# Reordering the head of an attention and MLP block: norms ahead of weight scaling, first keys on ScalarE, a shared bank for later keys, gate products as single steps

## The chip, the cores and the metric

The kernel runs on one core of one Trainium2 chip. The metric is device time in microseconds (us), the median of several executions. Before the change it was 1155.14 us (three runs, 1154.14 to 1156.71). The profiled span is about 2 us shorter than the device time of the same run (1153.5 us against 1155.31 for the kernel before).

## The reference, cut to what matters

One transformer block over 2048 tokens of 1024 channels, with adaptive layer norms, multi-query attention (32 query heads, one key and value head of 32 channels) and a gated MLP of width 3584.

```python
mod = (silu(c) @ w_mod).reshape(...)             # sa, ca, ga, sb, cb, gb: six rows of 1024
h = layernorm(x) * (1 + ca) + sa
q, k, v = h @ wq, h @ wk, h @ wv                  # k and v: one head for all 32 query heads
x = x + ga * (softmax(q k^T / sqrt(32)) v @ wo)
h = layernorm(x) * (1 + cb) + sb
x = x + gb * ((silu(h @ w1) * (h @ w3)) @ w2)
```

## The kernel before

The kernel builds a graph of instructions, each with a priority and a stated duration. A list scheduler in the program then fixes one static order for each engine, and picks a bank of PSUM (where the kernel's matmuls put their results) for each group. Copying a result out of PSUM is called evacuating it; a tile is 128 tokens. A lower priority number goes first, and `bp` below is subtracted from it.

The parts that the change and the argument touch:

```python
# eight PSUM banks: PB[0], PB[1], and six that the scores use (PB[2..7] = SP[0..5])
def kproj(t0, n, allow=None):                     # keys of n tokens, replicated on four row groups
    ...
    g = mm_group(NC, kmm, lambda c: [("WKS", 0)] + hk(c, t0, n), n_cols=n, allow=allow, mode="V", prio=KP)
    G.add("dve", lambda e, g=g: e.tensor_scalar(KT[:, sl], PB[g.bank][:, 0:n], BIA[:, 0:1], None, ALU.add), ...)

EV = (("act",), ("act",), ("dve",), ("dve",))     # who evacuates the transposes of tiles 0-3, 4-7, ...
def ln(t):
    bp = -3 if t >= 8 else 0                      # priority of a tile's statistics and norm
...
kproj(0, 256, (2, 3, 4, 5))
qproj(0, 256, 0, (2, 3, 4, 5), prio=1)
kproj(256, 256, (6, 7))
kproj(512, 512, (6, 7))                           # keys of tiles 4 to 7: in a bank of the scores
...
def gate(m, scale):                               # rows ga and gb, for all tokens: wide products
    ...
            def mm(e, kb=kb, sl=sl, g=g):
                for k in range(4):
                    i = e.matmul(PB[g.bank], SCB[kb * 4 + k], WMS[:, sl, k, :], ...)   # 128x512
            G.add("pe", mm, ..., dur=4 * MM, ...)
...                                               # columns sb and cb: 16 small products in one step
            def mm(e, kb=kb, h=h, sl=sl, g=g):
                for k in range(4):
                    for j in range(4):
                        i = e.matmul(PB[g.bank][:, h * 4 + j:h * 4 + j + 1], WMS[:, sl, k, j * P:(j + 1) * P], ...)
            G.add("pe", mm, ..., dur=16 * 0.06, ...)
...
def step(f, s):                                   # one score step: 4 heads x 256 keys x 256 queries
    parts = [(0, 2, 2 * ((2 * i) % 3), 2), (2, 2, 2 * ((2 * i + 1) % 3), 2)]   # its 4 score banks
    G.add("pe", smm, ...)                         # 8 matmuls, then two exponentials of 128x1024 on ScalarE
    G.add("act", ... e.activation(U[...], SP[:, b0:b0 + nb, 0:W], ACT.Exp, scale=SCALE), ...)
...
G.warm = (WARM, MM, warm, ident, 26.0)            # until WARM = 250 us: spare TensorE time is filled
```

The last line is about warm-up matmuls: where the scheduler sees TensorE idle, it inserts products with the identity matrix, whose results nobody reads; they are meant to keep TensorE's clock up.

The softmax here doesn't subtract the row's maximum and nothing guards it: scores larger than these inputs give would overflow.

## Time and profile before

| stretch | what bounds it |
|---|---|
| 0 to 34 us | loads (DMA share 1.09 from 14 to 24 us) and the chain to the first scores; ScalarE waits for keys |
| 34 to 1040 us | ScalarE's 1024 exponentials, TensorE about equally busy |
| 1036 to 1153 us | TensorE alone: the rest of one MLP, one output projection and one whole MLP |

There are 512 score steps, each followed by two exponentials. Below, "exponential n" is the n-th in time, and the "tail" runs from the start of the last score step to the end of the span.

Time by stretches, before. After the stretch and its length come each engine's busy time with its instruction count (PE is TensorE, PEld its weight loads, DVE VectorE, ACT ScalarE), then the granted TensorE clock, the DMA engines' share and GB/s.

```profile
150.00:200.00 50.00, 46.45 (x562) 19.78 (x560) 46.98 (x74) 47.09 (x51) 3.30 (x4) 0.97 0.06 18
300.00:350.00 50.00, 46.52 (x691) 28.38 (x683) 41.52 (x60) 48.69 (x54) 3.40 (x4) 0.97 0.70 176
350.00:1000.00 650.00, 644.81 (x9269) 444.40 (x9269) 607.99 (x879) 646.70 (x735) 12.20 (x20) 1.00 0.68 189
```

From 350 to 1000 us TensorE and ScalarE are both 99% busy. TensorE is less busy from 188 to 192 us (2.14 of 4) and from 330 to 335 us (1.67 of 5), and the mean clock of the two stretches of 50 us around these places drops to 0.97.

ScalarE's timeline in the head, before, with the start, the length, the instruction, and in brackets the idle time ahead of it and what ended it (L930 is line 930 of the kernel's source):

```profile
25.75 2.13 ACT L745 ACTIVATE WREG<-WO,MODC 128x384 bf16<-128x384 bf16 x4
27.79 1.91 ACT L930 ACTIVATE UREG<-SP 128x1024 bf16<-128x1024 f32 x2
33.66 12.09 ACT L930 ACTIVATE UREG<-SP 128x1024 bf16<-128x1024 f32 x13 [3.96 <-PE SP L920]
```

The first two exponentials run, then ScalarE waits 3.96 us for the second score step. TensorE's timeline in the same stretch:

```profile
27.03 0.40 PE L920 MATMUL SP<-QT,KT 32*128 32x256 bf16 x8
27.36 0.39 PE L637 MATMUL SP<-HREG,WKS 128*32 128x512 bf16 x1
28.99 0.40 PE L637 MATMUL SP<-HREG,WKS 128*32 128x512 bf16 x3 [1.24 <-issue]
29.32 0.75 PE L762 MATMUL PB<-SAB,WO 128*128 128x1 bf16 x24
29.93 0.35 PE L768 MATMUL PB<-QT,SAB 128*128 128x32 bf16 x8
30.21 1.69 PE L637 MATMUL SP<-HREG,WKS 128*32 128x512 bf16 x28
31.84 1.05 PE L658 MATMUL PB<-HREG,WREG 128*128 128x256 bf16 x8
...
33.21 0.40 PE L920 MATMUL SP<-QT,KT 32*128 32x256 bf16 x8
```

L920 is a score step, L637 keys, L762 and L768 bias products, L658 queries. Between the two score steps stand the keys of tiles 4 to 7 (L637, 512 columns), which occupy a score bank, and a gap of 1.24 us that no wait in the profile explains ("issue").

The place near 330 us, TensorE's timeline and two stretches, before:

```profile
330.48 0.40 PE L920 MATMUL SP<-QT,KT 32*128 32x256 bf16 x8
332.31 0.40 PE L920 MATMUL SP<-QT,KT 32*128 32x256 bf16 x8 [1.43 <-ACT UREG L930]
334.14 0.40 PE L920 MATMUL SP<-QT,KT 32*128 32x256 bf16 x8 [1.44 <-ACT UREG L930]
335.01 1.53 PE L1146 MATMUL PB<-QT,HREG 128*128 128x256 bf16 x9 [0.47 <-DVE QT L1129]
```

```profile
330.00:335.00 5.00, 1.67 (x46) 0.64 (x37) 5.00 (x14) 5.00 (x7) 0.00 (x0) 1.00 0.83 226
335.00:340.00 5.00, 4.99 (x40) 2.99 (x41) 3.50 (x4) 4.32 (x7) 0.00 (x0) 0.66 0.68 216
```

Two score steps have nothing else between them. TensorE is busy 1.67 of 5 us, and in the next 5 us the granted clock is 0.66. The trace's clock record has it at one half for exactly 3.413 us, from 335.6 to 339.0, also from 192.3 to 195.7, and again from 1151.4 to the end of the span.

### The profile page before, as it was taken

Reading aid. Unit: us, or ns where it says so; the run is one execution under the profiler, and the core shown is the slowest. Engines: PE = TensorE matmul, PEld = TensorE weight load, DVE = VectorE, ACT = ScalarE, POOL = GpSimd, SP = SyncE. Lnnn points to the kernel's source line nnn. Section 1 sums busy time; section 2 is a strip of 40 time slices with the busy share of each in tenths; the row PEclk is TensorE's granted clock in tenths of the full one; section 3 lists DMA queues with packets and bytes.
Section 4 is the critical chain, followed back from the end, with each engine's and each line's share of the span. In section 5 each row is a group of like instructions: output and inputs, shape, how many; then the busy total and the mean of one; then the engine's idle time right before and its main releaser. Section 6 shows DMA issues by size and latency. Waiting matters only on the chain.

```text
span 1153.5 us, 35455 instructions
## 1 busy us (share of the span) xinstructions
PE 1119.9 (97%) x15839; PEld 762.4 (66%) x15839; DVE 989.5 (86%) x1498; ACT 1026.0 (89%) x1170; POOL 39.0 (3%) x86
## 2 busy tenths in 40 slices
PE   7898998999989999999999999999999999999998
PEld 4564443766657766766677756776677667777887
DVE  6838899899889998999899998999899998997452
ACT  5899999999999999999999999999999999991110
POOL 4200001000000000000000000000000000000000
PEclk9999999999999999999999999999999999999999
DMA  9616101966586556955597647866696659757996
GB/s 330 216 29 202 39 1 48 291 186 180 150 204 192 158 155 168 271 171 163 143 262 200 179 134 207 237 171 175 151 262 177 173 147 245 214 158 192 291 290 159
DMA packets 385416, 211.09 MB, mean 183 GB/s; under 512 B 21744, under 2 KB 376048, under 8 KB 385264
## 3 DMA queue, kind: packets, MB, share of 16 engines
q1 hardware_dynamic: 383184, 208.69, 65.2%
q8 instruction: 125, 2.05, 0.8%
q10 hardware_dynamic: 2080, 0.13, 0.1%
q14 instruction: 27, 0.22, 0.1%
HBM read 201.46 MB, written 4.19 MB: 178 GB/s over the span
## 4 chain that ended last, share of the span: by engine, by line
PE 46%; ACT 45%; DVE 6%; issue 1%; SPq 1%; DMA 1%; POOL 0%
ACT UREG L930 41%; PE PB L1180 12%; PE SP L920 6%; PE PB L1146 5%; PE PB L980 5%; PE PB L658 4%; PE PB L1112 4%; PE SP L1180 4%; PE SP L1146 3%; ACT WREG L1155 2%; ACT GSB L1155 2%; DVE UREG L953 1%; DVE UREG L947 1%; PE PB L1007 1%; DMA UREG<-in_w_mod_dram 1%
## 5 line engine op out<-in xcount | busy, mean ns | idle before, releaser
L930 ACT ACTIVATE UREG<-SP 128x1024 bf16<-128x1024 f32 x1024 | 968.7, 1083 | 12.8 <-PE SP L920 10.8
L953 DVE TENSOR_TENSOR UREG<-UREG 128x2048 bf16<-128x2048 bf16 x240 | 292.2, 1218 | 10.4 <-ACT UREG L930 8.4
L920 PE MATMUL SP<-QT,KT 32*128 32x256 bf16 x4096 | 203.8, 273 | 10.9 <-ACT UREG L930 10.3
L1146 PE MATMUL PB<-QT,WREG 128*128 128x256 bf16 x1632 | 203.1, 273 | 0.6 <-DVE DSB L1031 0.2
L1146 PEld LDWEIGHTS PB<-QT,WREG 128*128 128x128 bf16 x1632 | 148.9, 98 | 44.7 <-issue 28.5
L947 DVE TENSOR_TENSOR UREG<-UREG 128x2048 bf16<-128x2048 bf16 x120 | 145.8, 1215 | 8.4 <-ACT UREG L930 7.1
L920 PEld LDWEIGHTS SP<-QT,KT 32*128 32x128 bf16 x4096 | 60.7, 92 | 134.2 <-ACT UREG L930 81.5
L1146 PE MATMUL PB<-QT,HREG 128*128 128x256 bf16 x1056 | 133.6, 275 | 1.3 <-DVE DSB L1031 0.6
L980 PE MATMUL PB<-UREG,V 128*32 128x256 bf16 x4096 | 127.4, 273 | 0.7 <-ACT UREG L930 0.5
L1146 PEld LDWEIGHTS PB<-QT,HREG 128*128 128x128 bf16 x1056 | 96.9, 98 | 30.7 <-issue 19.7
L980 PEld LDWEIGHTS PB<-UREG,V 128*32 128x32 bf16 x4096 | 101.6, 96 | 21.0 <-issue 14.8
L1180 PE MATMUL PB<-WREG,HREG 128*128 128x256 bf16 x728 | 92.6, 273 | 1.9 <-DVE HREG L1158 1.9
L1180 PEld LDWEIGHTS PB<-WREG,HREG 128*128 128x128 bf16 x728 | 66.9, 98 | 23.5 <-issue 13.8
L658 PE MATMUL PB<-HREG,WREG 128*128 128x512 bf16 (+1 forms) x312 | 66.2, 345 | 3.8 <-DVE QT L661 1.7
L1146 PE MATMUL PB<-QT,X 128*128 128x256 bf16 x544 | 67.9, 273 | 0.2
L1155 ACT ACTIVATE GSB<-GSB 128x512 bf16<-128x512 bf16 x56 | 39.6, 707 | 30.5 <-DVE GSB L1153 30.5
L962 DVE TENSOR_TENSOR UREG<-UREG 128x2048 bf16<-128x2048 bf16 x52 | 63.3, 1218 | 0.8
L1112 PE MATMUL PB<-WO,QT 128*128 128x512 bf16 x232 | 59.2, 381 | 0.0
L1146 PEld LDWEIGHTS PB<-QT,X 128*128 128x128 bf16 x544 | 50.3, 98 | 13.2 <-issue 7.8
L1180 PE MATMUL PB<-HREG 128*128 128x256 bf16 x448 | 57.3, 273 | 1.3 <-DVE HREG L1158 1.3
L1155 ACT ACTIVATE WREG<-WREG 128x512 bf16<-128x512 bf16 x56 | 40.1, 715 | 20.5 <-DVE WREG L1153 20.5
L1180 PEld LDWEIGHTS PB<-HREG 128*128 128x128 bf16 x448 | 41.0, 98 | 14.5 <-issue 8.9
(134 smaller groups left out, 1042.1 us busy)
## 6 DMA issues: line engine op xcount, KB each, us to landing
WREG<-in_B_w_dram SPq DMA_DIRECT2D x112, 512.0 KB, 5.1
HREG<-in_B_w_dram SPq DMA_DIRECT2D x74, 512.0 KB, 5.3
WREG<-in_B_w_dram SPq DMA_DIRECT2D x33, 896.0 KB, 5.2
X<-in_B_w_dram SPq DMA_DIRECT2D x38, 512.0 KB, 5.4
HREG<-in_B_w_dram SPq DMA_DIRECT2D x21, 896.0 KB, 5.1
X<-in_B_w_dram SPq DMA_DIRECT2D x10, 896.0 KB, 5.1
X<-in_A_x_dram SPq DMA_DIRECT2D x32, 256.0 KB, 5.9
WREG<-in_w_mod_dram SPq DMA_DIRECT2D x16, 512.0 KB, 4.5
```

Source lines behind the costliest of these rows:

```text
L658: g = mm_group(NC, lambda e, b, c: e.matmul(b[:, 0:n], WQ[:, c, f * P:(f + 1) * P], HT[:, c, sl], start=c == 0, stop=c == NC - 1), lambda ...
L920: r = e.matmul(SP[:, b, o:o + qn], KT[32 * gg:32 * gg + 32, kts[j] * P:(kts[j] + 1) * P], QT[32 * gg:32 * gg + 32, f, q0:q0 + qn], start=T ...
L930: G.add("act", lambda e, u=u, h0=h0, n=n, b0=b0, nb=nb: e.activation(U[:, u, h0 * W:(h0 + n) * W].rearrange("p (b w) -> p b w", b=nb), SP[ ...
L947: G.add("dve", lambda e, tr=tr, u=u, fu=first_u: e.tensor_tensor(TR[:, tr, 0:4 * W], U[:, fu, 0:4 * W], U[:, u, 0:4 * W], ALU.add), reads= ...
L953: G.add("dve", lambda e, tr=tr, u=u: e.tensor_tensor(TR[:, tr, 0:4 * W], TR[:, tr, 0:4 * W], U[:, u, 0:4 * W], ALU.add), reads=[("TR", tr) ...
L962: G.add("dve", lambda e, ta=ta, tb=tb: e.tensor_tensor(TR[:, ta, 0:4 * W], TR[:, ta, 0:4 * W], TR[:, tb, 0:4 * W], ALU.add), reads=[("TR", ...
L980: r = e.matmul(PB[g.bank][32 * gg:32 * gg + 32, 0:qn], V[:, kt, :], U[:, pu, (gg * npk + j) * qn:(gg * npk + j + 1) * qn], start=w0 + n == ...
L1007: r = e.matmul(PB[g.bank][32 * gg:32 * gg + 32, qn:2 * qn], SEL[:, ga, gj, :], a[:, (gg * npk + x % npk) * qn:(gg * npk + x % npk + 1) * q ...
L1112: g = mm_group(NC, lambda e, b, f, t=t, h=h: e.matmul(b, QT[:, f, t * P:(t + 1) * P], WO[:, f, h * 512:(h + 1) * 512], start=f == 0, stop= ...
L1146: return e.matmul(b[:, j * qn:(j + 1) * qn], w13[:, w, c, j * P:(j + 1) * P], QT[:, c, q0:q0 + qn], start=c == 0, stop=c == NC - 1)
L1155: G.add("act", lambda e, b=b: e.activation(TB[b], GS[b], ACT.Tanh, scale=0.5), reads=[("GS", b)], writes=[("TB", b)], clear=alias("TB") if ...
L1180: G.add("pe", lambda e, g=g, j=j, fc=fc, hf=hf, first=first, w2s=w2s: e.matmul(PB[g.bank][:, j * 256:(j + 1) * 256], HHT[:, hf * NH + fc, ...
```

## The change

The intent is to start the exponentials earlier: norms of tiles 4 to 7 come ahead of weight scaling, their evacuation is shared with VectorE, the first keys are evacuated by ScalarE with the bias, the keys of tiles 4 to 7 go to a bank that the scores do not use, and bias and gate products become single steps.

```diff
+        if t0 == 0:
+            G.add("act", lambda e, g=g: e.activation(KT[:, sl], PB[g.bank][:, 0:n], ACT.Identity, bias=BIA[:, 0:1]), ...
+            return
-    EV = (("act",), ("act",), ("dve",), ("dve",))
+    EV = (("act",), ("act", "dve"), ("dve",), ("dve",))
-        bp = -3 if t >= 8 else 0
+        bp = -3 if t >= 8 else 8
-        G.add("pe", qb, reads=["SAB", ("WQR", k)], dur=(f1 - f0) * NC * 0.027, lat=0.2, acq=g, ..., prio=0)
+        for f in range(f0, f1):
+            G.add("pe", lambda e, f=f: qb(e, f), ..., dur=NC * 0.027, ..., prio=0 if k == 0 else 1.5)
-            G.add("pe", vbmm, ..., prio=0)
+            G.add("pe", vbmm, ..., prio=1.5)
-    kproj(512, 512, (6, 7))
+    kproj(512, 512, (1,))
-                G.add("pe", mm, reads=SCBK + wms(sl), dur=4 * MM, ...)       # 4 wide gate products
+                for k in range(4):
+                    G.add("pe", ..., dur=MM, ...)                             # one each
-                G.add("pe", mm, reads=["SCT"] + wms(sl), dur=16 * 0.06, ...) # 16 modulation products
+                for k in range(4):
+                    G.add("pe", mm, ..., dur=4 * 0.027, ...)                  # four each
```

Cut: the priority of three small VectorE operations on the conditioning vector, from 0 to -9.

More of the change, by code (lines that the diff above doesn't have):

```diff
@@ L511, in build @@
     G.add("dve", lambda e: e.scalar_tensor_tensor(CT[:], CT[:], 1.0, CROW[:], ALU.add, ALU.mult),
-          reads=["CT", "CROW"], writes=["CT"], dur=0.25, prio=0)
+          reads=["CT", "CROW"], writes=["CT"], dur=0.25, prio=-9)
     G.add("dve", lambda e: e.tensor_scalar(SCR[:], CT[:], 0.5, None, ALU.mult), reads=["CT"], writes=["SCR"], dur=0.2,
-          prio=0)
+          prio=-9)
     g = grp()
@@ L518, in build @@
     G.add("dve", lambda e, g=g: e.tensor_copy(SCT[:], PBH[g.bank][:, 0:8]), writes=["SCT"], groups=[(g, "r")], dur=0.12,
-          prio=0)
+          prio=-9)
     for a in range(NC // 4):
@@ L640, in kproj @@
         g = mm_group(NC, kmm, lambda c: [("WKS", 0)] + hk(c, t0, n), n_cols=n, allow=allow, mode="V", prio=KP)
+        if t0 == 0:
+            G.add("act", lambda e, g=g: e.activation(KT[:, sl], PB[g.bank][:, 0:n], ACT.Identity, bias=BIA[:, 0:1]),
+                  reads=["BIAK"], writes=[("KT", t) for t in range(t0 // 256, (t0 + n) // 256)], groups=[(g, "r")],
+                  dur=act_t(n), prio=-5)
+            return
         G.add("dve", lambda e, g=g: e.tensor_scalar(KT[:, sl], PB[g.bank][:, 0:n], BIA[:, 0:1], None, ALU.add),
@@ L757, in bias, with qb @@
         g = grp(allow)
-        def qb(e):
-            for f in range(f0, f1):
-                for c in range(NC):
-                    r = e.matmul(PB[g.bank][:, f:f + 1], WO[:, c, f * P:(f + 1) * P], SAB[:, c:c + 1],
-                                 start=c == 0 and f == f0, stop=True, skip_group_check=True)
+        def qb(e, f):
+            for c in range(NC):
+                r = e.matmul(PB[g.bank][:, f:f + 1], WO[:, c, f * P:(f + 1) * P], SAB[:, c:c + 1],
+                             start=c == 0 and f == f0, stop=True, skip_group_check=True)
             return r
@@ L777, in kbmm @@
             return r
-        G.add("pe", qb, reads=["SAB", ("WQR", k)], dur=(f1 - f0) * NC * 0.027, lat=0.2, acq=g, groups=[(g, "w")],
-              mode="F", prio=0)
+        for f in range(f0, f1):
+            G.add("pe", lambda e, f=f: qb(e, f), reads=["SAB", ("WQR", k)], dur=NC * 0.027, lat=0.2,
+                  acq=g if f == f0 else None, groups=[(g, "w")], mode="F", prio=0 if k == 0 else 1.5)
         if kb:
@@ L784, in bias @@
         if vb:
-            G.add("pe", vbmm, reads=["SAB"] + WVK, dur=0.3, lat=0.2, groups=[(g, "w")], mode="F", prio=0)
+            G.add("pe", vbmm, reads=["SAB"] + WVK, dur=0.3, lat=0.2, groups=[(g, "w")], mode="F", prio=1.5)
             G.add("dve", lambda e: e.tensor_copy(VB[:], PB[g.bank][:, 16:48]), writes=["VB"],
@@ L839, in gate @@
                     ("wms", sl), writes=wms(sl), nbytes=P * 2048 * 2, after=[wo_load])
-                def mm(e, kb=kb, sl=sl, g=g):
-                    for k in range(4):
-                        i = e.matmul(PB[g.bank], SCB[kb * 4 + k], WMS[:, sl, k, :],
-                                     start=(kb == 0 and k == 0), stop=(kb == 1 and k == 3))
-                    return i
-                G.add("pe", mm, reads=SCBK + wms(sl), dur=4 * MM, lat=0.2, acq=g if kb == 0 else None,
-                      groups=[(g, "w")], mode="F")
+                for k in range(4):
+                    G.add("pe", lambda e, kb=kb, k=k, sl=sl, g=g: e.matmul(
+                        PB[g.bank], SCB[kb * 4 + k], WMS[:, sl, k, :], start=(kb == 0 and k == 0),
+                        stop=(kb == 1 and k == 3)), reads=SCBK + wms(sl), dur=MM, lat=0.2,
+                        acq=g if kb == 0 and k == 0 else None, groups=[(g, "w")], mode="F")
             G.add("dve", lambda e, g=g, h=h: e.tensor_scalar(GBB[:, h * 512:(h + 1) * 512], PB[g.bank], scale, None,
@@ L866, in build, with mm @@
                     ("wms", sl), writes=wms(sl), nbytes=P * 2048 * 2)
-                def mm(e, kb=kb, h=h, sl=sl, g=g):
-                    for k in range(4):
+                for k in range(4):
+                    def mm(e, kb=kb, h=h, sl=sl, g=g, k=k):
                         for j in range(4):
@@ L873, in mm @@
                                          skip_group_check=True)
-                    return i
-                G.add("pe", mm, reads=["SCT"] + wms(sl), dur=16 * 0.06, lat=0.2,
-                      acq=g if (h == 0 and kb == 0) else None, groups=[(g, "w")], mode="F")
+                        return i
+                    G.add("pe", mm, reads=["SCT"] + wms(sl), dur=4 * 0.027, lat=0.2,
+                          acq=g if (h == 0 and kb == 0 and k == 0) else None, groups=[(g, "w")], mode="F")
         a, b2 = ((1.0, 0.0), (1.0, 1.0))[m]
```

## The prediction

> **What bounds it now.** Time by stretches: from 350 to 1000 us ScalarE and TensorE are both about 99% busy. ScalarE's 1024 exponentials (968.7 us in the groups, 0.917 us apart) set the pace from 33.7 to about 1040 us; then TensorE alone works off about 110 us. Time is saved only by starting the exponentials earlier, closing ScalarE or TensorE gaps, or leaving less TensorE work for the tail. The change touches the head.
>
> **The head (timeline, chain of waits).** Loads gate TensorE until the last modulation products at 23.37. Bias products end at 24.97, key and query evacuations run 25.29 to 26.69, first scores at 27.03. The first two exponentials run 27.79 to 29.70; then ScalarE waits 3.96 us, the largest wait in its table, until 33.66: the second score step needs the banks that hold the keys of tiles 4 to 7. Those are finished only after an unexplained TensorE gap (27.75 to 28.99), 0.9 us of bias products, 1.6 us of key products and a 0.75 us VectorE evacuation.
>
> **Removed, added, moved.**
> 1. Shared bank: the second score step no longer waits for those bias products and that evacuation (main step). 28 of the 32 key products (0.058 us each) still stand before it. I expect the TensorE gap to recur (an instruction-queue packet is in flight just before it while DMA engines are full): second step at about 30.5, not 33.2; gain about 3 us; without the gap 4.2.
> 2. Norms first, evacuation of tiles 4 to 7 shared by VectorE (8 at 0.50 us now on ScalarE, until 25.75): it ends about 3 us earlier, but the load at 23.37 still gates: almost nothing directly. The two scale products (1.2 and 0.4 us) fall into VectorE's 3.6 us idle time.
> 3. First keys by ScalarE: first exponential 0 to 0.4 us earlier.
> 4. Single-step gate and bias products: same arithmetic, finer order. The order also has 9 fewer warm-up matmuls (1.9 us of TensorE).
>
> **Second effect.** The order differs later too. In before, two score steps near 330 us have no other TensorE work: TensorE idles 3.3 us (330 to 335), and the granted clock is 0.66 in 335 to 340. [...] In the new order block 1's output projection stands six steps earlier, and those steps are filled. Counting matmuls at their traced spacing, 106.2 us of TensorE work follow the last score step, not 109.6: another 3.4 us, if VectorE's norm chain keeps up.
>
> **Sum.** 3.3 (head) + 3.4 (tail) + 0.3 (ScalarE wait near 340), less 1 for new waits: 6 us. Predicted 1149.0 us, 1145.5 to 1152.5; faster by over 2%: 0.01, within: 0.98, slower: 0.01.
>
> **What would show it.** ScalarE's 3.96 us wait shrinks to about 1; second score step at about 30.5; transposes of tiles 4 to 7 begin near 19, not 20.9; last modulation products stay at 23.4; no idle stretch and no halved clock near 330; the stretch after ScalarE's end about 3 us shorter.
>
> **What would make it wrong.** The TensorE gap grows or moves before the first scores; TensorE, with less slack in 34 to 60 us, falls behind, so that exponentials wait and the 3 us are given back; a new idle stretch elsewhere with a halved clock; the 330 us chain stays late on VectorE, so the second effect is absent (then about 1152).

The remark on the TensorE gap is from the trace of before: a packet of 16384 bytes on an instruction queue (q8) lies there from 26.42 to 27.47 us, and the DMA engines' share is 1.06 from 24.0 to 27.5 us and 1.04 from 27.5 to 29.0.

## The result, and the profile after

The changed kernel took 1147.57 us (six runs, 1146.10 to 1149.34), the kernel before 1155.76 us in the same rounds (six runs, 1154.14 to 1156.73). The ratio is 0.993, 95% interval 0.9916 to 0.9944. Here and below, ratios and intervals are worked out from the runs of both kernels in the same rounds; they are not quite the ratio of the medians. The profiled run of the changed kernel (span 1144.2 us) was among its fastest.

Time by stretches, after:

```profile
150.00:200.00 50.00, 44.45 (x634) 20.71 (x634) 47.46 (x72) 48.80 (x53) 3.30 (x4) 1.00 0.14 37
300.00:350.00 50.00, 50.00 (x698) 33.57 (x696) 44.69 (x63) 49.59 (x56) 3.43 (x4) 1.00 0.83 205
350.00:1000.00 650.00, 646.91 (x9262) 442.58 (x9271) 603.78 (x879) 647.43 (x734) 17.15 (x20) 1.00 0.69 190
```

ScalarE's timeline in the head, after:

```profile
25.57 2.12 ACT L750 ACTIVATE WREG<-WO,MODC 128x384 bf16<-128x384 bf16 x4
27.60 1.92 ACT L933 ACTIVATE UREG<-SP 128x1024 bf16<-128x1024 f32 x2
30.21 9.30 ACT L933 ACTIVATE UREG<-SP 128x1024 bf16<-128x1024 f32 x10 [0.70 <-PE SP L923]
```

TensorE's timeline in the head, after (L923 is the score step now, L766 the bias products):

```profile
26.58 0.40 PE L923 MATMUL SP<-QT,KT 32*128 32x256 bf16 x8
26.91 0.40 PE L637 MATMUL PB<-HREG,WKS 128*32 128x512 bf16 x4
28.35 1.48 PE L637 MATMUL PB<-HREG,WKS 128*32 128x512 bf16 x24 [1.04 <-issue]
29.77 0.40 PE L923 MATMUL SP<-QT,KT 32*128 32x256 bf16 x8
30.09 0.40 PE L637 MATMUL PB<-HREG,WKS 128*32 128x512 bf16 x4
30.43 0.75 PE L766 MATMUL PB<-SAB,WO 128*128 128x1 bf16 x24
```

The second score step starts at 29.77 us instead of 33.21, behind 28 key products and a TensorE gap of 1.04 us. ScalarE's wait shrank from 3.96 to 0.70 us.

Near 330 us, after:

```profile
330.00:335.00 5.00, 5.00 (x61) 3.66 (x54) 4.73 (x7) 5.00 (x7) 0.00 (x0) 1.00 0.92 280
335.00:340.00 5.00, 5.00 (x58) 3.60 (x60) 4.96 (x7) 5.00 (x8) 0.00 (x0) 1.00 1.12 310
```

The idle stretch and the halved clock are gone. The last score step, before and then after:

```profile
1036.41 0.40 PE L920 MATMUL SP<-QT,KT 32*128 32x256 bf16 x8
```

```profile
1030.86 0.40 PE L923 MATMUL SP<-QT,KT 32*128 32x256 bf16 x8
```

From there to the end of the span it is 117.1 us before (1153.50 - 1036.41) and 113.4 us after (1144.24 - 1030.86). Of the 128x256 products with the MLP's first matrices (L1146), 482 start in this tail before and 450 after. At 0.109 us apart, the 32 fewer are about 3.5 us: the new order does them before the last score step.

To see where time is won or lost along the way, this table, worked out from the traces, gives the start of some exponentials: absolute for the kernel before, and the lead (minus) or lag (plus) against it for the others. The last columns give the tail and the mean granted clock over all runs of the kernel (31 runs for before, from the three sets of experiments).

| kernel | exp. 3 | exp. 17 | exp. 65 | exp. 101 | exp. 181 | exp. 321 | exp. 1024 | tail, us | clock |
|---|---|---|---|---|---|---|---|---|---|
| before | 33.66 | 46.45 | 92.70 | 126.48 | 205.93 | 344.11 | 1038.26 | 117.1 | 0.9948 |
| the change | -3.45 | -2.98 | -3.61 | -3.56 | -5.58 | -5.56 | -5.51 | 113.4 | 0.9980 |
| bank_only | -2.70 | -0.55 | -0.64 | +0.99 | +1.02 | +1.01 | +1.01 | 117.1 | 0.9936 |
| gate_only | +1.58 | +1.57 | +1.13 | +1.47 | +0.93 | +0.91 | +0.97 | 113.4 | 0.9976 |
| bank_and_gate | -2.51 | -0.37 | -0.88 | -0.52 | -2.65 | -2.67 | -2.61 | 113.4 | 0.9990 |
| all_but_gate | -3.62 | -3.16 | -3.00 | -0.46 | -2.22 | -1.54 | -1.54 | 117.1 | 0.9937 |
| all_but_bank | -2.32 | -1.14 | -1.68 | -1.04 | -1.57 | -1.58 | -1.35 | 113.4 | 0.9968 |
| all_but_bias | -3.47 | -1.64 | -2.15 | -0.81 | -1.33 | -1.34 | -1.29 | 113.6 | 0.9984 |
| act_delay | -0.55 | +0.71 | +0.08 | +1.78 | -0.22 | -0.20 | -0.12 | 113.4 | 0.9962 |

The whole change wins 3.45 us by exponential 3, keeps about 3 to 3.6 until exponential 101, wins 2.0 more by exponential 181, and 3.7 us in the tail: 5.6 at the last score step (1036.41 - 1030.86) + 3.7 = 9.3 us of span between these two profiled runs, 8.2 us between the medians. One row is one execution, so halved clock windows that fall in one run and not in another are in it. Two stretches can be read across all the traces:

- **Exponentials 101 to 181.** The three rows of the gate edit's order with a halved window near 192 us, as in before (gate_only, all_but_bank, all_but_bias), gain 0.5 us here; the three without one (the change, bank_and_gate, act_delay) gain 2.0 to 2.1. So about 1.5 of the change's 2.0 us are that window, which this run did not have, and 0.5 is the order.
- **Exponentials 181 to 321.** The lead does not grow. The change first loses 0.95 us up to exponential 311 (lead 4.63) and then wins 0.93 near 330 us; the other five rows with the gate edit do the same. In the exponentials the filled steps near 330 thus leave no net gain against before.

### The profile page after: what moved, and what is told of

It reads as the page before. It is cut to its first block, busy times and chain, and to the rows that moved or that the text cites. A ratio compares the mean times of both kernels' runs of the same rounds, so it can differ in the third digit from the quotient of the medians.

```text
span 1144.2 us, 35491 instructions
## 1 busy us (share of the span) xinstructions
PE 1114.2 (97%) x15800; PEld 758.0 (66%) x15830; DVE 985.3 (86%) x1501; ACT 1024.9 (90%) x1167; POOL 43.6 (4%) x86
## 4 chain that ended last, share of the span: by engine, by line
PE 84%; ACT 9%; DVE 4%; POOL 1%; issue 1%; DMA 0%; SPq 0%
PE PB L1149 30%; PE PB L1183 16%; PE SP L923 12%; PE PB L983 10%; ACT UREG L933 8%; PE PB L1115 4%; PE SP L1149 3%; PE PB L663 3%; PE SP L1183 2%; PE PB L1010 2%; DVE UREG L956 1%; DVE QT L666 1%; DVE UREG L950 1%; DVE ST L530 0%; POOL RS L553 0%
## 5 line engine op out<-in xcount | busy, mean ns | idle before, releaser
L1149 PE MATMUL PB<-QT,WREG 128*128 128x256 bf16 x1648 | 206.8, 273 | 2.0 <-DVE DSB L1034 2.0
L923 PE MATMUL SP<-QT,KT 32*128 32x256 bf16 x4096 | 203.5, 273 | 4.9 <-ACT UREG L933 4.7
L923 PEld LDWEIGHTS SP<-QT,KT 32*128 32x128 bf16 x4096 | 60.8, 92 | 128.4 <-ACT UREG L933 75.4
L983 PEld LDWEIGHTS PB<-UREG,V 128*32 128x32 bf16 x4032 | 98.1, 96 | 26.6 <-issue 17.7
L1183 PE MATMUL PB<-WREG,HREG 128*128 128x256 bf16 x812 | 100.6, 273 | 0.0
L1183 PEld LDWEIGHTS PB<-WREG,HREG 128*128 128x128 bf16 x812 | 75.5, 98 | 19.9 <-issue 11.0
L1183 PE MATMUL PB<-HREG 128*128 128x256 bf16 x532 | 67.3, 273 | 0.0
L663 PE MATMUL PB<-HREG,WREG 128*128 128x512 bf16 (+1 forms) x299 | 61.5, 338 | 3.7 <-DVE QT L666 1.6
L1158 ACT ACTIVATE GSB<-GSB 128x512 bf16<-128x512 bf16 x56 | 39.7, 709 | 27.5 <-DVE GSB L1156 27.5
L551 POOL TENSOR_SCALAR RS<-MV 128x1 f32<-128x1 f32 x32 | 20.6, 649 | 1004.2 <-DVE MV L532 1004.0
L1183 PEld LDWEIGHTS PB<-HREG 128*128 128x128 bf16 x532 | 49.3, 98 | 13.7 <-issue 7.8
```

The lines of the kernel that those rows point to most:

```text
L663: g = mm_group(NC, lambda e, b, c: e.matmul(b[:, 0:n], WQ[:, c, f * P:(f + 1) * P], HT[:, c, sl], start=c == 0, stop=c == NC - 1), lambda ...
L923: r = e.matmul(SP[:, b, o:o + qn], KT[32 * gg:32 * gg + 32, kts[j] * P:(kts[j] + 1) * P], QT[32 * gg:32 * gg + 32, f, q0:q0 + qn], start=T ...
L983: r = e.matmul(PB[g.bank][32 * gg:32 * gg + 32, 0:qn], V[:, kt, :], U[:, pu, (gg * npk + j) * qn:(gg * npk + j + 1) * qn], start=w0 + n == ...
L1149: return e.matmul(b[:, j * qn:(j + 1) * qn], w13[:, w, c, j * P:(j + 1) * P], QT[:, c, q0:q0 + qn], start=c == 0, stop=c == NC - 1)
L1158: G.add("act", lambda e, b=b: e.activation(TB[b], GS[b], ACT.Tanh, scale=0.5), reads=[("GS", b)], writes=[("TB", b)], clear=alias("TB") if ...
L1183: G.add("pe", lambda e, g=g, j=j, fc=fc, hf=hf, first=first, w2s=w2s: e.matmul(PB[g.bank][:, j * 256:(j + 1) * 256], HHT[:, hf * NH + fc, ...
```

## The experiments

Theory at the start: the shared bank gives the head's gain, the gate edit gives the late order and the tail, and the two add up. Rivals: the early start alone moves everything behind it, or the single steps bring nothing. All kernels gave correct results.

### The shared bank alone (bank_only)

```diff
-    kproj(512, 512, (6, 7))
+    kproj(512, 512, (1,))
```

> The kernel before with only the shared bank for the keys of tiles 4 to 7. Its instruction order on TensorE is that of before except that the second score step stands ahead of the bias products. Theory (bank gives the head, the gate steps give the late order): second score step near 30.5 us instead of 33.2, ScalarE's 3.96 us wait about 1.2; still 109.6 us of TensorE work after the last score step, still the idle stretch near 330; in all about 3 us faster, 1152.5. Rival (the earlier head alone moves everything that follows, the late order is a consequence): about 8 us faster, 1147.5.

Measured: 1156.86 us against 1156.22, ratio 1.0001 (0.9989 to 1.0013). Both theories missed. TensorE's timeline, bank_only:

```profile
30.51 0.40 PE L920 MATMUL SP<-QT,KT 32*128 32x256 bf16 x8
30.84 1.48 PE L637 MATMUL PB<-HREG,WKS 128*32 128x512 bf16 x24
32.25 1.05 PE L658 MATMUL PB<-HREG,WREG 128*128 128x256 bf16 x8
33.23 0.40 PE L920 MATMUL SP<-QT,KT 32*128 32x256 bf16 x8
```

The bank does what was meant: exponential 3 leads by 2.70 us. (The expectation misread the order: the bias products still stand ahead of the second score step, and 24 of the key products behind it.) By exponential 17 only 0.55 us is left. The third score step stands behind those 24 key products and a query projection and starts 2.7 us after the second (33.23 and 30.51), while two exponentials take 1.83. The rest goes between exponentials 65 and 101. In the profiled run the clock stood at one half for 6.8 us there (101.4 to 108.2; its mean from 100 to 150 us is 0.93); how much of that loss is the clock is not shown. The tail is unchanged.

### The gate steps alone (gate_only)

The two hunks on gate and modulation products of the diff above, and nothing else.

> The kernel before with only the gate and modulation products as single steps (which also carry a shorter duration in the scheduler). The head is unchanged: second score step at 33.2, ScalarE wait 3.96 us. The order after about 87 us is the new one: no two score steps without other work near 330, 106.2 us of TensorE work after the last score step. Theory: about 5 us faster, 1150.5, all of it after 150 us. Rival (the single steps add nothing by themselves, as the prediction said in its point 4): 1155.5, same as before.

Measured: 1151.23 us against 1156.22, ratio 0.9959 (0.9948 to 0.9971). So 5.0 us come from the part to which the prediction gave no gain of its own. The tail is 113.4 us, 3.7 less than before, and there is no idle stretch near 330. The head is not faster: in the profiled run it is even 1.58 us later, with a halved clock from 30.6 to 34.0 (its mean from 24 to 34 us is 0.83).

### Both of these (bank_and_gate)

> The kernel before with the shared bank and the single gate steps, without the norm order, the shared evacuation, ScalarE's first keys and the single bias steps. Theory (these two parts are all that matters): about 1147.5 to 1148.5, as the whole change. Rival (norms and evacuation matter for the head): 2 us or more slower than the whole change.

Measured: 1148.93 us against 1156.22, ratio 0.9941 (0.9929 to 0.9953). Two parts bring 7.3 us. The bank, worth nothing alone, brings 2.3 us on top of the gate steps (1151.23 - 1148.93, same chip and rounds). Against the whole change (ratio 0.9930, other rounds) about 1.3 us remain for the other parts. The two intervals overlap widely, so this can be told neither from nothing nor from the 2 us that the rival asked for.

### Everything but the gate steps (all_but_gate)

> The whole change without the single gate steps. 109.6 us of TensorE work after the last score step, two score steps near 330 us without other work. Theory: head gain of about 3.5 us kept, the rest lost: 1152. Rival (late gain comes from the early start): 1147.5.

Measured: 1156.07 us against 1156.22, ratio 1.0006 (0.9992 to 1.002). A miss: a lead of 3.6 us at exponential 3 and 3.0 at exponential 65 ends in no gain at all in the median (the profiled run, the fastest of six, kept 1.5 us). The table shows where it goes: 2.5 us between exponentials 65 and 101, and the tail is that of before. The waits between 86 and 130 us, first ScalarE's, then TensorE's; the columns are the total, the number of times and the longest:

```profile
ACT UREG L935 <- PE SP L925: 2.8, 5, 1.5
```

```profile
PE PB L663 <- DVE QT L666: 1.8, 1, 1.8
```

The same for the whole change:

```profile
ACT UREG L933 <- PE SP L923: 0.5, 2, 0.3
```

```profile
PE PB L663 <- DVE QT L666: 0.8, 2, 0.5
```

VectorE's timeline at that place, all_but_gate and then the change. L860 and L858 are the scaling of the output weights by the gate, L666 is the query evacuation:

```profile
98.99 4.30 DVE L860 TENSOR_TENSOR WO<-WO,GBB 128x1024 bf16<-128x1024 bf16 x7
103.21 0.74 DVE L666 TENSOR_SCALAR QT<-PB,BIA 128x512 bf16<-128x512 f32 x1
```

```profile
98.55 0.75 DVE L666 TENSOR_SCALAR QT<-PB,BIA 128x512 bf16<-128x512 f32 x1
99.21 3.69 DVE L858 TENSOR_TENSOR WO<-WO,GBB 128x1024 bf16<-128x1024 bf16 x6
```

Without the gate steps seven weight scalings (4.30 us) stand ahead of a query evacuation that TensorE needs. With them the evacuation is placed ahead of the last six. This is read from the traces; no run changed that order alone.

### A delay put back at the head (act_delay)

```diff
+    if i == 0 and h == 1:                 # after the second exponential
+        for d in range(7):
+            if d:
+                e.wait_ge(JSEM, d)
+            e.activation(JUNK[:], ..., ACT.Identity).then_inc(JSEM, 1)
```

> The whole change, same order on every engine, with seven small idle activations put on ScalarE right after the second exponential, so that the third one starts about 3.5 us later, near its old place (33.7). Theory 1 (in the new order ScalarE's start carries through to the end): about 3 us slower than the change, 1150.5, every exponential after the first few late by about 3. Theory 2 (TensorE's total work and gaps set the end; an early start alone is absorbed, as the shared bank alone was): less than 1 us slower, the lateness gone by exponential 200.

Measured: 1151.41 us against 1156.10, ratio 0.9964 (0.9952 to 0.9976), so 3.9 us slower than the change by the ratios (0.0034 of 1156; with the two intervals about 2 to 6). Exponential 3 starts at 33.12, 2.9 us later than in the change. Exponential 17 is 3.7 and exponential 181 is 5.4 us later. The lag grows by 0.8 us between exponentials 3 and 17 and by 1.7 between 65 and 101, and a halved window of this trace lies in each of the two (34.2 to 37.6 and 109.3 to 112.7 us); that they are the cause was not tested. With the new order the start does carry to the end. Theory 2 falls for this order, though it describes the old one.

### Everything but the bank (all_but_bank)

> The whole change without the shared bank. Head as before (third exponential near 33.5), late order new. If the head counts in the new order: 2.5 to 3.5 us slower than the change, about 1150.5, like the gate steps alone (1151.2). If the head does not count: 1148.

Measured: 1149.94 us against 1156.10, ratio 0.9952 (0.9941 to 0.9964), 2.5 us slower than the change by the ratios (with the two intervals about 0.5 to 4.5). The time is as expected, the way there is not: exponential 3 started at 31.35, not 33.5. In its trace only 8 of the 24 bias products stand ahead of the second score step (30.89 us). Beside the other parts the bank moves it by only 1.1 us, and raises the lead at exponential 17 from 1.14 to 2.98 us.

### Only more warm-up matmuls (before_warm_longer)

```diff
-    WARM = 250.0
+    WARM = 420.0
```

> The kernel before with warm-up matmuls allowed until 420 us of the scheduler's time instead of 250. The only difference in any engine's order is 4 + 4 warm-up matmuls in the two score steps near 330 us that had no other work. No useful work moves. Theory (the halved clock after that idle stretch is part of the loss): the halved window near 335 is gone, mean clock up by about 0.0015 to 0.003, time about 1 to 1.7 us shorter, 1154.8. Rival (the clock does not matter, only the missing work does): 1156.2, same as before.

Measured: 1154.30 us against 1156.10, ratio 0.9985 (0.9973 to 0.9997). The two stretches near 330 us in this kernel:

```profile
330.00:335.00 5.00, 4.52 (x84) 1.98 (x76) 5.00 (x11) 4.86 (x6) 0.00 (x0) 1.00 1.11 212
335.00:340.00 5.00, 4.08 (x50) 2.75 (x51) 4.22 (x8) 5.00 (x7) 0.00 (x0) 1.00 0.78 231
```

Eight matmuls that compute nothing kept the clock at 1.00. In this trace the exponentials start late (a halved window from 29.8 to 33.2 us in the head), but their lag against before falls from 1.30 us at exponential 311 to -0.21 at exponential 321, a gain of 1.5 us. So the clock is part of what is won near 330, not only the work that fills the steps.

### The wide gate products alone (gate_split_only), and the stated duration alone (mod_dur_only)

```diff
 # gate_split_only: four wide gate products as single steps, modulation products as before
 # mod_dur_only:
-                G.add("pe", mm, reads=["SCT"] + wms(sl), dur=16 * 0.06, ...)
+                G.add("pe", mm, reads=["SCT"] + wms(sl), dur=16 * 0.027, ...)
```

> The kernel before with only the 16 wide gate products (128x512) as single steps; the modulation products stay in groups of 16 with their old stated duration (0.96 us, where 16 of them take about 0.4 us in the trace). Read from the order: TensorE's late order is still the old one, with two empty score steps near 330 and 109.6 us of work after the last score step; with the shorter stated duration added, every engine's order becomes exactly that of gate_only. Theory (the order, not the finer steps themselves, brings the 5 us): 1155 to 1156, as before. Rival (finer steps let TensorE fill gaps): 1151.

> The kernel before with only one number changed: the scheduler's stated duration of a group of 16 modulation products, 0.43 us instead of 0.96. No instruction is added or removed on purpose but the order changes: thin score steps at 151 and 171 instead of 155 and 156, still 109.6 us of TensorE work after the last score step. Theory (what counts is the work left after the last score step and the idle stretches, and both parts of the gate edit are needed): within 2 us of before, 1155. Rival (the corrected duration alone is the cause): 1151.

Measured, both against 1155.91 us: gate_split_only 1157.14 us, ratio 1.0008 (0.9996 to 1.0021); mod_dur_only 1155.99 us, ratio 0.9994 (0.9981 to 1.0008). Neither half of the gate edit gains anything, and their tails are 117.1 and 118.0 us. Both halves together, even with the modulation products left in groups of 16, give the order of gate_only on every engine; that was compared in the built programs, where the order and the operands of every engine's instructions are the same, not run. So, on the kernel before, finer modulation steps are not needed for the 5 us. What is needed is the order that the scheduler finds with single wide products and the shorter stated duration.

### Everything but the single bias steps (all_but_bias)

The whole change with the 24 bias products in one step of priority 0, and the value bias at priority 0.

> The whole change with the bias products of queries 1 to 3 in one group of 24 again. Order on TensorE: second score step ahead of 24 key products and a query projection, so the third step comes about 2.6 us after the second, more than the 1.83 us that its two exponentials take. Theory (the bias split is what lets the early start last): third exponential near 30, but about 2 us of the 3 us lead gone by exponential 16; 1.5 us slower than the change, 1149. Rival (norm order and shared evacuation keep the lead): lead of 3 us kept at exponential 16, 1147.6.

Measured: 1149.12 us against 1155.91, ratio 0.9938 (0.9926 to 0.9950). The point estimate is 0.9 us slower than the change (0.0008 of 1156), which the intervals do not separate. The head is clear: exponential 3 leads by 3.47 us as in the change, exponential 17 by only 1.64 instead of 2.98. The single bias steps keep the lead that the bank makes, together with their later priority (1.5 instead of 0), which this run put back too.

### The TensorE gap (warm_split, warm_page)

```diff
-                r = e.matmul(PB[b], IDENT[:], IDENT[:].unsqueeze(1).broadcast_to([P, 4, P]), ...)
+                for q in range(4):                       # warm_page: not for the first two
+                    r = e.matmul(PB[b][:, q * P:(q + 1) * P], IDENT[:], IDENT[:], ...)
```

In before and in the change the gap comes right after the 705th TensorE instruction of the trace (matmuls, weight loads and the few semaphore instructions all counted), although different work precedes it. The same holds for all twelve traces with whole warm-up matmuls.

> The whole change with each warm-up matmul of 512 columns issued as four of 128: same time for them, 198 more TensorE instructions, 198 of them or fewer ahead of the first scores. In before and in the change the TensorE gap ahead of the second score step comes after the same count of TensorE instructions in the trace (705). Theory (instruction fetch): the gap at the keys of tiles 4 to 7 disappears or comes some 190 instructions earlier in the work; ScalarE's remaining 0.70 us wait before its third exponential goes; 0 to 0.7 us faster, 1147. Rival (a wait on data or banks at that place): the gap stays ahead of the second score step, about 1.0 us.

> As warm_split, but with the first two warm-up matmuls left whole, so that TensorE has 186 instructions more ahead of the first scores, not 198. In ten traces the gap came after instruction 705, in warm_split after 961 = 705 + 256, in the middle of the second score step. Theory (instructions are fetched 256 at a time[...]): the gap is again after instruction 961, which now lies behind the second score step; ScalarE's wait before its third exponential goes from 0.7 or 0.8 us to 0.1 or less. The time is at most 0.8 us shorter, 1147. Rival: the gap moves elsewhere or ScalarE still waits 0.7 us.

The split warm-up matmuls do take the same time: eight of 128 columns 0.62 us in warm_split (17.34), two of 512 columns 0.61 us in before (17.31).

Measured: warm_split 1148.15 us (ratio 0.9933, 0.9920 to 0.9946), warm_page 1147.24 us (ratio 0.9926, 0.9912 to 0.9940). Neither can be told from the change by time. TensorE's timeline, warm_split and then warm_page:

```profile
26.93 1.69 PE L637 MATMUL PB<-HREG,WKS 128*32 128x512 bf16 x28
28.68 0.29 PE L923 MATMUL SP<-QT,KT 32*128 32x256 bf16 x4
29.99 0.29 PE L923 MATMUL SP<-QT,KT 32*128 32x256 bf16 x4 [1.03 <-issue]
```

```profile
28.66 0.40 PE L923 MATMUL SP<-QT,KT 32*128 32x256 bf16 x8
28.99 0.39 PE L637 MATMUL PB<-HREG,WKS 128*32 128x512 bf16 x2
29.92 0.39 PE L637 MATMUL PB<-HREG,WKS 128*32 128x512 bf16 x2 [0.54 <-issue]
```

ScalarE's timeline in warm_page:

```profile
27.61 3.73 ACT L933 ACTIVATE UREG<-SP 128x1024 bf16<-128x1024 f32 x4
31.61 7.71 ACT L933 ACTIVATE UREG<-SP 128x1024 bf16<-128x1024 f32 x8 [0.27 <-PE SP L923]
```

In warm_split the gap stands after instruction 961 = 705 + 256, in the middle of the second score step, so the wait stayed and that part of its expectation missed. Moved by 12 instructions more, as warm_page does, it falls behind that step: the four first exponentials run without a break and exponential 3 leads by 4.25 us. By exponential 17 the lead is 3.17, hardly more than the change's 2.98, because ScalarE waits for later score steps (0.27 us for the third, 0.32 us for one at 39.65). This supports instruction fetch in blocks of 256 as the cause of the gap; which work stands there does not matter. The DMA records agree: a packet of 16384 bytes on an instruction queue ends at 27.47 us in before, 26.88 in the change, 28.68 in warm_split and 28.53 in warm_page, and TensorE goes on 1.3 to 1.5 us after it each time.

## Why the prediction was right, and where it was not

The time and the range were right: 1147.57 us against 1149.0, in 1145.5 to 1152.5. The mechanism in the head and in the tail was read correctly, but the prediction named the bank as the main step and no edit as the cause of the late order. That the size came so near (6 us forecast, 8.2 measured) is partly luck, as the last two points show.

- **Head.** Predicted 3.3 us, second score step near 30.5, ScalarE's wait about 1. Measured: 3.45 us at exponential 3 and 2.98 at exponential 17, second step at 29.77, wait 0.70. The TensorE gap recurred as expected (1.04 us), and warm_page shows what it cost: exponential 3 could start 0.8 us earlier, with no gain that the time shows.
- **Other signs.** Transposes of tiles 4 to 7 begin at 19.36 us in the change (predicted near 19), and the last modulation products stay at 23.42.
- **Tail and second effect.** Predicted 3.4 us from counting matmuls after the last score step; measured 3.7. The idle stretch and the halved clock near 330 are gone. before_warm_longer shows that the clock there is worth about 1.5 us in its trace and 0.0015 of the time (0.0003 to 0.0027). In the change the place wins 0.93 us, but the order loses as much on the way there, so nothing of it is left in the lead at exponential 321, nor of the 0.3 us entered for a wait near 340.
- **The step that failed is point 4**, "Single-step gate and bias products: same arithmetic, finer order", with no gain entered for it. The gate part alone is the largest single gain, 5.0 us; without it the whole change shows no gain (ratio 1.0006, 0.9992 to 1.002). The prediction saw the late order in the built program but did not build the single parts, which would have shown which edit makes it: the builds with the whole gate edit have the short tail, those without any of it do not.
- **Point 1, "main step", holds only together with others.** The shared bank alone gained nothing; on top of the gate steps 2.3 us. In the old order its lead was used up by the work put off (exponentials 3 to 17) and between exponentials 65 and 101, where its trace also has a halved clock.
- **The term "less 1 for new waits" had the wrong sign.** No net loss followed: the lead grew by 2.0 us between exponentials 101 and 181. About 1.5 of the 2.0 us are the halved window near 192 us, which the profiled run of the change does not have (clock 1.00 from 150 to 200 us) and traces of other kernels with the same late order do (gate_only, 0.97 there; all_but_bank; all_but_bias): their exponentials gain only 0.5 us between 101 and 181. That part differs from run to run.

What stays open: the shares of the norm order, the shared evacuation, ScalarE's first keys and the three priorities, which together with the bias steps are about 1.3 us beyond bank and gate, not told apart from nothing; and how much of the whole gain is fewer halved windows. The mean clock rose from 0.9948 to 0.9980, but only the window near 335 was tested by itself. An estimate from the record: over its 99 runs, each kernel against its own mean, a run is about 0.7 us longer for each 0.001 of mean clock that it loses, so 0.0032 would be some 2.4 of the 8.2 us.

## What to carry to other kernels

Where a program's scheduler fixes the order, treat a stated duration as part of the kernel: build each part of a change by itself and compare the order far from the edit, above all the work left after the bottleneck engine's last instruction. An early start is worth something only if the next few steps and every later place where engines wait for each other can use it, so follow the lead over the loop, step by step, rather than at its first step. Where two engines are both 99% busy, look for the few steps in which one has nothing to do: filling them, even with matmuls that compute nothing, saved the clock here (1.00 instead of 0.66 near 335 us).

## What these traces show of the TensorE gap and of the clock

- **Gap.** It stands after TensorE instruction 705 in before and in the change, and after 961 = 705 + 256 once 198 or 186 more instructions precede. The queue with the packets of 16384 bytes (q8) carried 125 of them in before, for 31950 TensorE instructions, and 124 in the change, for 31907: about one for every 256. At all 124 other places in before's trace that lie a multiple of 256 instructions away from 705, the step to the next instruction is 0.22 us or less; at 705 it is 1.63 us, and 1.43 in the change. The DMA engines' share is 1.04 there (27.5 to 29.0 us, before) and 1.05 (26.9 to 28.4 us, the change); that this is the reason was not tested. TensorE went from instruction 449 to 705 in 4.2 us (22.69 to 26.92 us, the change) and then stood for 1.4 us between two instructions, 5.7 us after passing instruction 449; in before it was 6.1 us.
- **Clock.** The two halved windows inside before's trace last 3.413 us each; in bank_only one lasts 6.8 us (101.4 to 108.2). From 330 to 335 us of before TensorE was busy 1.67 of 5 us, with no single idle stretch over 1.44 us, and from 335.6 the clock was halved; with 4.52 of 5 us busy (before_warm_longer) it was not. No threshold comes out of these traces: in the 3.41 us ahead of the two halved windows of before TensorE was busy for 1.49 us (188.85 to 192.26) and 1.41 us (332.21 to 335.62), and in the change a stretch hardly less thin, 1.58 us busy from 101.62 to 105.03, was not followed by a halved window.
- **Clock and time.** The mean clock goes with most of the spread within one kernel: 31 runs of before had mean clocks of 0.993 to 0.999 and times of 1153.90 to 1158.18 us; the eight at 0.993 took 1156.10 or more, the seven at 0.996 1155.34 or less. Kernels that differ by less than 1% are therefore compared with the clock of each run beside its time.
